# Softmax rows divided after the product with v instead of before it, with the reciprocals spread by way of DRAM

## The chip, the cores and the metric

One NeuronCore of a Trainium2 chip runs the whole program. The metric is device time in microseconds (us) of one execution; a lower time is better. Five engines work side by side, each through its own queue in order: PE (TensorE, matrix products and transposes), DVE (VectorE), ACT (ScalarE), POOL (GpSimd) and SP (SyncE, which here issues every DMA). They wait for each other by semaphores. PE writes to eight PSUM banks; the other engines copy out of them into SBUF, and POOL works on SBUF alone.

## What is computed

Attention with a mask by blocks of 64, a token mixer, a channel mixer and a gated mixer follow each other, on 4 batches of 576 rows and 512 columns (8 heads of 64).

```python
def _attn_ref(q, k, v):
    scores = scale * np.matmul(q, k.transpose(0, 1, 3, 2))
...
    mask = block_i >= block_j
    scores = np.where(mask, scores, -1000000000.0)
    scores = scores - np.max(scores, axis=-1, keepdims=True)
    attn = np.exp(scores)
    attn = attn / (np.sum(attn, axis=-1, keepdims=True) + 1e-09)
    return np.matmul(attn, v).astype(np.float32)

def _moe_ref(x, w_tok1, w_tok2, w_ch1, w_ch2):
    xt = x.transpose(0, 2, 1)
    h = np.maximum(xt @ w_tok1, 0.0) @ w_tok2
    u = x + h.transpose(0, 2, 1)
    h2 = np.maximum(u @ w_ch1, 0.0) @ w_ch2
    return (u + h2).astype(np.float32)

def _moe2_ref(x, mu_k, mu_r, w_k, w_v, w_r):
...
    k = np.maximum(xk @ w_k, 0.0)
    v = k * k @ w_v
    r = 1.0 / (1.0 + np.exp(-(xr @ w_r)))
    return (r * v).astype(np.float32)
```

## The kernel before

**Attention** goes by 16 pairs of heads, p = 0 to 15; four pairs make a batch, and two pairs are one token unit (b, g). For each pair PE computes the scores in three steps (`emit_s`, operands from the tile z, half of the array's rows for each head), and the mask by blocks lets the five row blocks i have 64, 192, 320, 448 and 576 columns (`KE`). For each head h and row block i:

- `m` on DVE (line 389) adds the mask, takes the row maximum and writes the scores to the SBUF tile P;
- `e` on ACT (line 394) takes the exponential in place, and the row sums go to the small tile st;
- `rc` on DVE (lines 398 and 399), four times in a pair, adds 1e-9 to two or three columns of sums and takes the reciprocals;
- `n` on POOL (line 403) multiplies P by the reciprocals, ten times in a pair.

Then PE transposes P in 128x128 pieces, in six groups (`t`, lines 412 and 414; 25 transposes in a pair), ACT or DVE copies each group to a tile pt, and PE multiplies with v in two passes (`pv`, half of the array's columns for each head). Two copies (`q`) bring the result, already with channels on the partitions, into u.

**Token mixer.** For each of the eight units, PE transposes u (`xt`, line 668), ACT and DVE split it into a rounded part and a rest (xnh, xnl), and PE multiplies twice (`k1` by w1, `k2` by w2) with the rectifier between them; `ku` on DVE (line 742) adds the result to u.

**Channel mixer and gated mixer.** Products L and O by w_ch1 and w_ch2 (tiles xhl, hpA, hpB), and then K, R and V (tiles named pair) follow. Their weights are unpacked on ACT, DVE and POOL while the stages before them run; of the pages of w_ch1 and w_ch2 the trace names the raw tiles `raw` and `rawx` and the decoded tiles `td` and `w`.

**What sets the order.** `Plan` takes every step with its engine, a cost, its dependencies and a due time, and records them one by one in the order in which its own reckoning would start them; each engine's queue then holds them in that order. The numbers in the table `TILT` shift the due times by kind of step. Where a step may go to one of two engines (`("ACT", "DVE")`), the plan chooses. Rings limit what is alive at once: `dense` gives three PSUM banks to `pv`, `xt`, `k1` and `k2` together, `pt` two to the transposes of P, `cs` three to the scores.

At the start PE runs twelve products on a zero tile (`warm`), and sixteen more of them (`fill`, tile wz) stand where the plan found PE without other work; all of them are always run.

```python
add(("n", p, h, i), "POOL", 0.31 + 0.00085 * KE[i], [("rc", p, h, g)], ...)
add(("t", p, g), "PE", ..., tprev + [("n", p, h, i) for h, i in need] + ["begin"], ...)
prev = [("q", 4 * b + 2 * g + k, part) for k in range(2) for part in range(2)]   # of xt
```

Of the kernel before, what the change touches and what calls it, by code (L numbers as in the profile page):

```python
# [27 lines left out]
NP = B * H // 2  # L28
# [38 lines left out]
class Plan:  # L67
# [7 lines left out]

    TURNS = {"rc", "d2", "vs", "vs2", "lo", "xm", "xsl", "xT", "Y", "TS", "VL", "KS"}

# [129 lines left out]
def attn_mixer_rwkv_kernel(ctx: ExitStack, tc: tile.TileContext, z, v, vl, wt1, wt2, wc1, wc2, wk, wv, wr, mu, out):  # L207
# [28 lines left out]
    def c_pool2(n):  # L236
        return 0.2 + 0.0023 * n
# [6 lines left out]
    def c_dma(n):  # L244
        return n / 170e3
# [64 lines left out]
    def begin():  # L310
        DVE.memset(f32(wz), 0.0)  # L311
        DVE.memset(eps, 1e-9)
# [17 lines left out]
    plan.ring("z", 2)  # L330
    plan.ring("st", 6)
    plan.ring("cd", 1)
# [12 lines left out]
    def load_v(p):  # L345
        SP.dma_start(out=vs[p % 3], in_=v[p])
        for h in range(2):
            k = slice(64 * h, 64 * h + 64)
            SP.dma_start(out=vd[p % 3][k, :, k], in_=vl[p, k])

# [27 lines left out]
    def p_view(p, h, i):  # L378
        o = (128 * i + 64) * h
        return tl["P", p, i][:, o:o + KE[i]]  # L380

    def emit_max(p, h, i):

        m = mask[:, 0:64] if i == 0 else mask[:, S - KE[i]:S] if h == 0 else mask[:, 512:512 + KE[i]]
        if ("P", p, i) not in tl:
            tl["P", p, i] = pbuf[i][plan.slot[f"P{i}", ("P", p, i)]]
        if ("st", p, h) not in tl:
            tl["st", p, h] = att3.tile([128, 3, 8], F32, tag="st", bufs=6, name="st")
        DVE.tensor_tensor_reduce(p_view(p, h, i), s_view(p, h, i), m, -0.125, 3.0e38, ALU.add, ALU.min,  # L389
                                 tl["st", p, h][:, 0, i:i + 1])  # L390

    def emit_exp(p, h, i):
        st, w = tl["st", p, h], p_view(p, h, i)
        ACT.activation(w, w, ACTF.Exp, bias=st[:, 0, i:i + 1], scale=-1.0, accum_out=st[:, 1, i:i + 1])  # L394
# [26 lines left out]
    def emit_pv(p, chunks):  # L421
        vt, vx = vs[p % 3], vd[p % 3]
        for i in chunks:
            part = int(i == 0)
            if ("pv", p, part) not in tl:
                tl["pv", p, part] = bank(("pv", p, part))
            t, o = tl["pv", p, part], max(0, 128 * i - 128)
            for j in range(i + 1):
                for h in range(2):
                    hs = slice(64 * h, 64 * h + 64)  # L430
                    if j < i:
                        g, c = OFF[h, i, j]
                        mm(t[hs, o:o + 128], vt[:, i - 1 - j if h else j, hs], tl["T", p, g][:, c:c + 128], j == 0, False)
                    else:
                        g, c = DIAG[i]
                        mm(t[hs, o + 64:o + 128] if i else t[hs, 0:64], vx[:, i, hs], tl["T", p, g][:, c:c + 64], j == 0, True)
# [18 lines left out]
    for p in range(NP):  # L455
        w = p - 3
        add(("z", p), "SP", c_dma(128 * 2 * S * 4), ["begin"] if p else [], lambda e, p=p: load_z(p), p - 5, alloc=[("z", ("z", p))], lat=2.0)
# [8 lines left out]
        for h in range(2):  # L466
            for i in range(5):
                step = 2 if i in (1, 2) else (h if i == 4 else 1 - h)
                key = ("c", p, h, {0: 3, 1: 2}.get(i, i))
                f = p - 1.9 + 0.1 * step + 0.03 * {4: 0, 3: 1, 0: 2, 2: 0, 1: 1}[i] + 0.01 * h  # L470
                first = (h, i) in ((0, 4), (1, 3))
                sk, pk = ("st", p, h), ("P", p, i)

                ahead = h == (0 if i in (4, 2, 1) else 1)
                add(("m", p, h, i), "DVE", 0.23 + 0.00104 * KE[i], [("s", p, step)] + ([] if first else [("m", p, h, 4 if h == 0 else 3)]) + ([] if ahead else [("m", p, 1 - h, i)]),
                    lambda e, p=p, h=h, i=i: emit_max(p, h, i), f,
                    alloc=[(f"P{i}", pk)] * ahead + [("st", sk)] * first, uses=[key] + [sk] * (not first) + [pk] * (not ahead))
                add(("e", p, h, i), "ACT", 0.48 + 0.00088 * KE[i], [("m", p, h, i)], lambda e, p=p, h=h, i=i: emit_exp(p, h, i), f, uses=[sk, pk])
                g = 1 if i >= 3 else 0
                add(("n", p, h, i), "POOL", 0.31 + 0.00085 * KE[i], [("rc", p, h, g)], lambda e, p=p, h=h, i=i: emit_norm(p, h, i),  # L480
                    p - 1.4 + 0.1 * (4 - i) + 0.01 * h, uses=[pk, sk])
            for g, (a, b) in enumerate(((0, 3), (3, 5))):
                add(("rc", p, h, g), "DVE", 0.36, [("e", p, h, i) for i in range(a, b)],
                    lambda e, p=p, h=h, a=a, b=b: emit_rec(p, h, a, b), p - 2.5, uses=[("st", p, h)])
# [378 lines left out]

    add("x1", "NONE", 0.0, [("q", NP - 1, 0), ("q", NP - 1, 1)] + [("q", p, k) for p in range(NP) for k in range(2)], change1, -99)
    add("x2s", "NONE", 0.0, ["x1"] + last_tok, change2s, -99)
# [80 lines left out]
    for t in range(NX):  # L946
# [22 lines left out]
        for f in range(12):  # L969
# [11 lines left out]
            def Ll(e, t=t, f=f, w=w):  # L981
# [364 lines left out]
```

## Time and profile before

| what | us |
|---|---|
| median of three executions | 759.02 |
| lowest and highest | 758.59 and 759.62 |
| the profiled execution, its own time | 759.16 |
| its span (first to last instruction) | 757.1 |
| between span and own time | 2.06 |

The profile is of one execution. Busy time is summed by engine; PE's matrix products are pipelined, so that the next starts before the one ahead has ended, and the end that the trace gives is modelled. What a product costs in a row of them is therefore the step from one start to the next, not its own duration. PEld is the load of the operand that stays in the array; it runs beside the products. Idle time of an engine is put down to what ended it (the releaser). A difference of 0.2% of the time, 1.5 us, is about what a measurement of this kernel can tell from none.

### The profile page before, as it was taken

How to read it: one execution, taken by the hardware profiler on the slowest of the kernel's cores; microseconds unless marked ns; L12 is line 12 of the kernel's file. 1: busy time of each engine (PE TensorE's matmuls, PEld its weight loads, DVE VectorE, ACT ScalarE, POOL GpSimd, SP SyncE). 2: the span in 40 equal slices, each digit the busy share in tenths (PEclk: the TensorE clock that was granted, in tenths of full speed). 3: DMA queues.
4: the chain of work that ended last, by engine and by line, in shares of the span. 5: the costliest groups of instructions: out<-in, count | busy, mean ns of one | idle time of the engine just before them, and what ended most of it. 6: DMA issues, size and time to landing. Idle time of an engine off the chain costs nothing.

```text
span 757.1 us, 14545 instructions
## 1 busy us (share of the span) xinstructions
PE 748.8 (99%) x5452; PEld 695.7 (92%) x5452; DVE 532.1 (70%) x1144; ACT 398.9 (53%) x863; POOL 277.7 (37%) x347
## 2 busy tenths in 40 slices
PE   9999999999999999999999999999999999999997
PEld 7888899999999888888888988889999999999997
DVE  5897888878486677557468465112798898897894
ACT  5887775876543461242242422110776775776772
POOL 5776867666475555244144220000120120110210
PEclk9999999999999999999999999999999999999999
DMA  6443544231013542726544550644845955946911
GB/s 197 120 129 115 141 118 153 85 117 58 29 56 134 174 139 83 249 94 221 209 151 169 196 195 29 212 149 156 305 151 189 325 205 186 328 140 186 332 45 48
DMA packets 53237, 119.56 MB, mean 158 GB/s; under 512 B 15408, under 2 KB 19504, under 8 KB 53168
## 3 DMA queue, kind: packets, MB, share of 16 engines
q1 hardware_dynamic: 53168, 118.64, 46.8%
q8 instruction: 43, 0.70, 0.4%
q14 instruction: 26, 0.21, 0.1%
HBM read 94.38 MB, written 24.25 MB: 157 GB/s over the span
## 4 chain that ended last, share of the span: by engine, by line
PE 98%; DVE 1%; POOL 1%; ACT 0%; issue 0%; DVEq 0%; POOLq 0%
PE bank L225 61%; PE pair L225 30%; PE bank L412 5%; PE bank L668 1%; PE bank L414 1%; POOL P L403 1%; ACT pt L215 0%; ACT P L394 0%; DVE u L1266 0%; DVE u L1261 0%; DVE xnl L686 0%; DVE xnh L217 0%; DVE pt L217 0%; DVE wz L311 0%; DVE u L742 0%
## 5 line engine op out<-in xcount | busy, mean ns | idle before, releaser
L225 PE MATMUL pair<-xhl,w 128*128 128x288 f32 x1296 | 176.5, 295 | 0.0
L225 PEld LDWEIGHTS pair<-xhl,w 128*128 128x128 f32 x1296 | 173.7, 188 | 0.6
L225 PE MATMUL bank<-xhl,w 128*128 128x460 f32 (+1 forms) x480 | 104.1, 371 | 0.0
L403 POOL TENSOR_SCALAR P<-P,st 128x448 f32<-128x448 f32 (+4 forms) x160 | 83.8, 546 | 47.5 <-DVE st L399 16.1
L225 PEld LDWEIGHTS bank<-xhl,w 128*128 128x128 f32 x480 | 90.0, 188 | 10.2
L394 ACT ACTIVATE P<-P,st 128x576 f32<-128x576 f32 (+4 forms) x160 | 88.4, 557 | 13.9 <-DVE st L389 13.5
L225 PE MATMUL bank<-hpB,w 128*128 128x460 f32 (+1 forms) x432 | 95.4, 372 | 0.0
L225 PEld LDWEIGHTS bank<-hpB,w 128*128 128x128 f32 x432 | 81.1, 188 | 9.6
L389 DVE CUSTOM_DVE_ANT_0 P<-bank,mask 128x576 f32<-128x576 f32 (+4 forms) x160 | 70.5, 483 | 15.8 <-PE bank L225 13.7
L535 POOL TENSOR_TENSOR td<-td,raw 128x512 int32<-128x512 int32 (+2 forms) x37 | 45.4, 1226 | 68.8 <-DVE td L531 45.9
L979 ACT ACTIVATE hpB<-bank 128x460 fp32r<-128x460 f32 (+1 forms) x36 | 20.0, 556 | 94.0 <-PE bank L225 94.0
L225 PE MATMUL bank<-hpA,w 128*128 128x460 f32 (+1 forms) x288 | 63.9, 371 | 0.0
L225 PEld LDWEIGHTS bank<-hpA,w 128*128 128x128 f32 x288 | 54.0, 188 | 6.2
L982 DVE SCALAR_TENSOR_TENSOR hpB<-bank,hpB 128x460 fp32r<-128x460 f32 (+1 forms) x36 | 22.9, 636 | 49.6 <-ACT hpB L979 49.6
L225 PE MATMUL bank<-z 64*128 64x224 f32 (+4 forms) x448 | 55.3, 376 | 0.0
L982 DVE SCALAR_TENSOR_TENSOR hpA<-bank,hpA 128x460 fp32r<-128x460 f32 (+1 forms) x24 | 15.3, 636 | 55.3 <-ACT hpA L979 55.3
L225 PE MATMUL bank<-xhl,wx 128*128 128x460 f32 (+1 forms) x240 | 53.3, 371 | 0.0
L225 PEld LDWEIGHTS bank<-z 64*128 64x128 f32 x448 | 44.6, 186 | 9.0 <-issue 3.8
L225 PEld LDWEIGHTS bank<-xhl,wx 128*128 128x128 f32 x240 | 45.1, 188 | 5.2
L412 PE MATMUL bank<-ident,P 128*128 128x128 f32 x320 | 49.2, 279 | 0.4 <-DVE pt L217 0.4
L979 ACT ACTIVATE hpA<-bank 128x460 fp32r<-128x460 f32 (+1 forms) x24 | 13.3, 555 | 64.7 <-PE bank L225 64.7
L215 ACT COPY pt<-bank 128x448 f32<-128x448 f32 (+1 forms) x61 | 32.9, 560 | 27.1 <-PE bank L412 12.4
(202 smaller groups left out, 1447.0 us busy)
## 6 DMA issues: line engine op xcount, KB each, us to landing
w<-pages SPq DMA_DIRECT2D x96, 512.0 KB, 4.6
pages<-raw SPq DMA_DIRECT2D x40, 256.0 KB, 2.5
z<-in_z SPq DMA_DIRECT2D x16, 576.0 KB, 3.8
raw<-in_wc SPq DMA_DIRECT2D x18, 512.0 KB, 3.6
pages<-rawx SPq DMA_DIRECT2D x30, 256.0 KB, 2.3
vs<-in_v SPq DMA_DIRECT2D x16, 256.0 KB, 3.8
out<-u SPq DMA_DIRECT2D x14, 288.0 KB, 3.7
rawx<-in_wc SPq DMA_DIRECT2D x6, 512.0 KB, 4.5
```

The source lines that it names most:

```text
L215: ACT.copy(o, i)
L225: PE.matmul(o, lhsT=l, rhs=r, start=start, stop=stop, skip_group_check=more)
L389: DVE.tensor_tensor_reduce(p_view(p, h, i), s_view(p, h, i), m, -0.125, 3.0e38, ALU.add, ALU.min, tl["st", p, h][:, 0, i:i + 1])
L394: ACT.activation(w, w, ACTF.Exp, bias=st[:, 0, i:i + 1], scale=-1.0, accum_out=st[:, 1, i:i + 1])
L403: POOL.tensor_scalar(w, w, tl["st", p, h][:, 2, i:i + 1], 1.0, ALU.mult, ALU.mult)
L412: PE.transpose(t[:, o + 128 * k:o + 128 * k + 128], tl["P", p, i][:, c:c + 128], ident)
L414: PE.transpose(t[:, 64 * k:64 * k + 128], tl["P", p, i][:, 128 * i:128 * i + 128], ident)
L535: POOL.tensor_tensor(td.bitcast(I32), td.bitcast(I32), lw, ALU.add)
L668: PE.transpose(t[0:rows, 256 * k + 128 * p:256 * k + 128 * p + 128], u[b][:, 2 * g + p, c:c + rows], ident)
L979: ACT.activation(tl["h", t, f][0], tl["lb", t, f][:, 0:w], ACTF.Relu)
L982: DVE.scalar_tensor_tensor(tl["h", t, f][1], tl["lb", t, f][:, 0:w], 0.0, f32(tl["h", t, f][0]), ALU.max, ALU.subtract)
```

## The change

P is no longer multiplied by the reciprocals. Transposes of P wait for the exponentials alone. The ten columns of sums of a pair (two heads, five row blocks) lie in one tile st. Once all ten exponentials are done, PE transposes these ten columns (`sx`, one transpose, in a bank of the ring `dense`) into ten rows of 128 numbers; DVE adds 1e-9 and takes the reciprocals (`rc`, lines 405 and 406, 10x128 each); SP writes the ten rows to a DRAM tensor `sums` (`rw`, line 409) and reads them back twice (`rr`, line 415), for each head a row of 576 numbers into 64 partitions of the tile rwide; and u of the pair is multiplied by rwide (`nq`, line 420, 128x576, on POOL or DVE), behind the copies `q`. The token mixer's transposes of u wait for `nq` of both pairs, and so does the start of the channel mixer's buffers (`x1`). To make room, v has two buffers in place of three, and a v load waits for the products of two pairs ahead. Of the numbers in `TILT` nearly all are other ones, so the order changes in all stages; the products L of the first slice keep to four banks from the third on.

```diff
-    eps = att.tile([128, 5], F32, name="eps")
...
-    vs = [att2.tile([128, 4, 128], F32, name=f"vs{s}") for s in range(3)]
-    vd = [att2.tile([128, 5, 128], F32, name=f"vd{s}") for s in range(3)]
+    vs = [att2.tile([128, 4, 128], F32, name=f"vs{s}") for s in range(2)]
+    vd = [att2.tile([128, 5, 128], F32, name=f"vd{s}") for s in range(2)]
+    rrow = [att2.tile([10, 128], F32, name=f"rrow{s}") for s in range(2)]
+    rwide = [att2.tile([128, S], F32, name=f"rwide{s}") for s in range(2)]
...
-    def emit_rec(p, h, a, e):
-        st = tl["st", p, h]
-        DVE.tensor_tensor(st[:, 2, a:e], st[:, 1, a:e], eps[:, a:e], ALU.add)
-        DVE.reciprocal(st[:, 2, a:e], st[:, 2, a:e])
-
-    def emit_norm(p, h, i):
-        w = p_view(p, h, i)
-        POOL.tensor_scalar(w, w, tl["st", p, h][:, 2, i:i + 1], 1.0, ALU.mult, ALU.mult)
+    def emit_row(p):
+        t = tl["sx", p] = bank(("sx", p))
+        PE.transpose(t[0:10, 0:128], tl["st", p][:, 1].rearrange("p h i -> p (h i)"), ident)
+
+    def emit_rec(p):
+        w = tl["rw", p] = rrow[plan.slot["rw", ("rw", p)]]
+        DVE.tensor_scalar(w, tl["sx", p][0:10, 0:128], 1e-9, 1.0, ALU.add, ALU.mult)
+        DVE.reciprocal(w, w)
+
+    def put_rec(p):
+        SP.dma_start(out=sums[p].rearrange("h (i c) -> (h i) c", c=128), in_=tl["rw", p])
+
+    def get_rec(p):
+
+        w = tl["rb", p] = rwide[plan.slot["rb", ("rb", p)]]
+        for h in range(2):
+            SP.dma_start(out=w[64 * h:64 * h + 64], in_=sums[p, h, 64:640].unsqueeze(0).broadcast_to([64, S]))
+
+    def emit_norm(p, e):
+        b, hp = divmod(p, 4)
+        w = u[b][:, hp, 1:1 + S]
+        (POOL if e == "POOL" else DVE).tensor_tensor(w, w, tl["rb", p], ALU.mult)
...
-            add(("t", p, g), "PE", 0.11 * (len(diag) + len(off)), tprev + [("n", p, h, i) for h, i in need] + ["begin"],
+            add(("t", p, g), "PE", 0.11 * (len(diag) + len(off)), tprev + [("e", p, h, i) for h, i in need] + ["begin"],
...
-            prev = [("q", 4 * b + 2 * g + k, part) for k in range(2) for part in range(2)]
+            prev = [("nq", 4 * b + 2 * g + k) for k in range(2)]
...
-                L, p0 + 0.5 * f, alloc=[("dense" if t == 0 else "lo4", key)], uses=[("x", "c", t), ("W", "c1", f)], lat=0.3)
+                L, p0 + 0.5 * f, alloc=[("dense" if t == 0 and f < 2 else "lo4", key)], uses=[("x", "c", t), ("W", "c1", f)], lat=0.3)
```

What the engines' queues hold, at three places. First PE, near the start, in pair 0 (z: scores, ident with P: transposes of P, st: the sums, pt with vs: products with v). Before:

```order
L412 MATMUL bank_128<-ident,P_95 128x128 x4
L412 MATMUL bank_127<-ident,P_95 128x128 x4
L225 MATMUL bank_130<-z 128x288
L225 MATMUL bank_126<-z 128x224
L225 MATMUL bank_130<-z 128x288
L225 MATMUL bank_126<-z 128x224
L225 MATMUL bank_126<-z 128x64
L412 MATMUL bank_124<-ident,P_93 128x128 x3
```

The same queue after, where the sums of pair 0 stand:

```order
L431 MATMUL bank_128<-ident,P_90 128x128
L401 MATMUL bank_129<-ident,st 10x128
L225 MATMUL bank_131<-z 128x288
L225 MATMUL bank_126<-z 128x224
L225 MATMUL bank_131<-z 128x288
L225 MATMUL bank_126<-z 128x224
L225 MATMUL bank_126<-z 128x64
L429 MATMUL bank_125<-ident,P_95 128x128 x4
L225 MATMUL bank_129<-pt_100,vs_108 64x128
```

Before, eight transposes stand together between scores; after, four stand between scores and products with v, and the transpose of the sums ends a visit.

Next DVE, in the pairs 2 to 4 (st: sums, td: unpacking of weights). Before:

```order
L217 COPY pt_98<-bank_125 128x512
L398 TENSOR_TENSOR st<-st,eps 128x3
L399 RECIPROCAL st<-st 128x3
L398 TENSOR_TENSOR st<-st,eps 128x3
L399 RECIPROCAL st<-st 128x3
L389 ISA P_91,st<-bank_126,mask 128x320
```

After, with the multiplication of u of pair 2:

```order
L548 SCALAR_TENSOR_TENSOR td<-raw,td 128x256
L217 COPY u_58<-bank_125 128x512
L217 COPY u_58<-bank_127 128x64
L420 TENSOR_TENSOR u_58<-u_58,rwide_114 128x576
L392 ISA P_90,st<-bank_129,mask 128x320
L392 ISA st 128x1
```

The small steps on the sums are gone from between the maxima, and a multiplication that needs a DMA's result stands ahead of the maxima of pair 4.

Last SP, in the pairs 1 to 3. Before:

```order
L343 DMA z<-in_z 128x1152
L346 DMA vs_110<-in_v 128x512
L349 DMA vd_113<-in_vl 64x5x64 x2
L547 DMA raw<-in_wt 64x256 x2
L346 DMA vs_111<-in_v 128x512
```

After:

```order
L346 DMA z<-in_z 128x1152
L409 DMA sums<-rrow_113 10x128
L415 DMA rwide_115<-sums 64x576 x2
L564 DMA raw<-in_wt 128x256
L349 DMA vs_109<-in_v 128x512
```

A write that waits for DVE, and two reads that wait for this write, now stand ahead of the loads.

## Rows read from the trace of the kernel before

**Rows 1.** The page: span, busy time of each engine, PE's granted clock in 40 slices.
```profile
span 757.1 us, 14545 instructions
...
PE 748.8 (99%) x5452; PEld 695.7 (92%) x5452; DVE 532.1 (70%) x1144; ACT 398.9 (53%) x863; POOL 277.7 (37%) x347
...
PEclk9999999999999999999999999999999999999999
```

**Rows 2.** Busy by stretch: length, then PE, PEld, DVE, ACT, POOL, clock, DMA share, GB/s.
```profile
0.00:216.00 216.00, 212.57 (x2254) 191.87 (x2255) 165.54 (x607) 152.65 (x450) 141.82 (x239) 1.00 0.37 110
```

**Rows 3.** PE in order of time (start, us, what), around its first and last stall.
```profile
18.50 2.10 PE L225 MATMUL bank<-z 64*128 64x320 f32 x18
...
20.53 1.05 PE L412 MATMUL bank<-ident,P 128*128 128x128 f32 x6
21.84 0.55 PE L414 MATMUL bank<-ident,P 128*128 128x128 f32 x3 [0.26 <-POOL P L403]
...
211.97 0.28 PE L225 MATMUL bank<-xnh,w1l 128*128 128x256 f32 x1
212.80 0.39 PE L225 MATMUL bank<-xnh,w1h 128*128 128x256 f32 x1 [0.55 <-DVE u L742]
```

**Rows 4.** PE in order of time from 61.67 to 68.32 us.
```profile
61.67 0.49 PE L412 MATMUL bank<-ident,P 128*128 128x128 f32 x3
61.99 0.27 PE L414 MATMUL bank<-ident,P 128*128 128x128 f32 x1
62.10 0.60 PE L412 MATMUL bank<-ident,P 128*128 128x128 f32 x4
62.46 0.36 PE L225 MATMUL bank<-xnh,w1h 128*128 128x256 f32 x1
62.66 0.28 PE L225 MATMUL bank<-xnl,w1h 128*128 128x256 f32 x1
62.78 0.28 PE L225 MATMUL bank<-xnh,w1l 128*128 128x256 f32 x1
...
65.50 1.23 PE L225 MATMUL bank<-z 64*128 64x288 f32 x10
66.67 0.66 PE L412 MATMUL bank<-ident,P 128*128 128x128 f32 x4
67.26 1.13 PE L225 MATMUL bank<-z 64*128 64x320 f32 x8
68.32 0.88 PE L225 MATMUL bank<-pt,vs 128*64 128x128 f32 x12
```

**Rows 5.** Groups of DVE by shape, and of POOL on the page: busy us, mean ns, idle.
```profile
L398 DVE TENSOR_TENSOR st<-st,eps 128x3 f32<-128x3 f32 x32 | 6.9, 215 | 0.1
L399 DVE RECIPROCAL st<-st 128x3 f32<-128x3 f32 x32 | 5.6, 176 | 1.1
L1046 DVE TENSOR_TENSOR xhl<-raw,xhl 128x576 fp32r<-128x576 f32 x26 | 19.6, 753 | 13.9 <-ACT xhl L215 13.9
...
L403 POOL TENSOR_SCALAR P<-P,st 128x448 f32<-128x448 f32 (+4 forms) x160 | 83.8, 546 | 47.5 <-DVE st L399 16.1
```

**Rows 6.** DMA issues: count, KB each, median us from issue to landing.
```profile
pages<-raw SPq DMA_DIRECT2D x40, 256.0 KB, 2.5
z<-in_z SPq DMA_DIRECT2D x16, 576.0 KB, 3.8
...
out<-u SPq DMA_DIRECT2D x4, 144.0 KB, 1.8
raw<-in_wt SPq DMA_DIRECT2D x2, 128.0 KB, 2.5
mu_sb<-in_mu SPq DMA_DIRECT2D x1, 4.0 KB, 3.5
```

**Rows 7.** The first load of z on PE, in order of time.
```profile
6.75 1.06 PEld L225 LDWEIGHTS bank<-z 64*128 64x128 f32 x10 [0.54 <-issue]
```

More of the change, by code (lines that the diff above doesn't have):

```diff
@@ L311, in begin @@
         DVE.memset(f32(wz), 0.0)
-        DVE.memset(eps, 1e-9)
         DVE.memset(f32(w1l[64:128, 4]), 0.0)
@@ L330, in attn_mixer_rwkv_kernel @@
     plan.ring("z", 2)
-    plan.ring("st", 6)
+    plan.ring("st", 3)
+    plan.ring("rw", 2)
+    plan.ring("rb", 2)
+    sums = nc.dram_tensor("sums", (NP, 2, 640), F32).ap()
     plan.ring("cd", 1)
@@ L345, in load_v @@
     def load_v(p):
-        SP.dma_start(out=vs[p % 3], in_=v[p])
+        SP.dma_start(out=vs[p % 2], in_=v[p])
         for h in range(2):
             k = slice(64 * h, 64 * h + 64)
-            SP.dma_start(out=vd[p % 3][k, :, k], in_=vl[p, k])
+            SP.dma_start(out=vd[p % 2][k, :, k], in_=vl[p, k])
     def s_part(p, h, i, cut):
@@ L386, in emit_max @@
             tl["P", p, i] = pbuf[i][plan.slot[f"P{i}", ("P", p, i)]]
-        if ("st", p, h) not in tl:
-            tl["st", p, h] = att3.tile([128, 3, 8], F32, tag="st", bufs=6, name="st")
+        if ("st", p) not in tl:
+            tl["st", p] = att3.tile([128, 2, 2, 5], F32, tag="st", bufs=3, name="st")
         DVE.tensor_tensor_reduce(p_view(p, h, i), s_view(p, h, i), m, -0.125, 3.0e38, ALU.add, ALU.min,
-                                 tl["st", p, h][:, 0, i:i + 1])
+                                 tl["st", p][:, 0, h, i:i + 1])
     def emit_exp(p, h, i):
-        st, w = tl["st", p, h], p_view(p, h, i)
-        ACT.activation(w, w, ACTF.Exp, bias=st[:, 0, i:i + 1], scale=-1.0, accum_out=st[:, 1, i:i + 1])
-    def emit_rec(p, h, a, e):
-        st = tl["st", p, h]
-        DVE.tensor_tensor(st[:, 2, a:e], st[:, 1, a:e], eps[:, a:e], ALU.add)
-        DVE.reciprocal(st[:, 2, a:e], st[:, 2, a:e])
-    def emit_norm(p, h, i):
-        w = p_view(p, h, i)
-        POOL.tensor_scalar(w, w, tl["st", p, h][:, 2, i:i + 1], 1.0, ALU.mult, ALU.mult)
+        st, w = tl["st", p], p_view(p, h, i)
+        ACT.activation(w, w, ACTF.Exp, bias=st[:, 0, h, i:i + 1], scale=-1.0, accum_out=st[:, 1, h, i:i + 1])
+    def emit_row(p):
[15 more added lines that the diff above has]
+        (POOL if e == "POOL" else DVE).tensor_tensor(w, w, tl["rb", p], ALU.mult)
     def emit_t(p, g):
@@ L421, in emit_pv @@
     def emit_pv(p, chunks):
-        vt, vx = vs[p % 3], vd[p % 3]
+        vt, vx = vs[p % 2], vd[p % 2]
         for i in chunks:
@@ L455, in attn_mixer_rwkv_kernel @@
     for p in range(NP):
-        w = p - 3
+        w = p - 2
         add(("z", p), "SP", c_dma(128 * 2 * S * 4), ["begin"] if p else [], lambda e, p=p: load_z(p), p - 5, alloc=[("z", ("z", p))], lat=2.0)
@@ L470, in attn_mixer_rwkv_kernel @@
                 f = p - 1.9 + 0.1 * step + 0.03 * {4: 0, 3: 1, 0: 2, 2: 0, 1: 1}[i] + 0.01 * h
-                first = (h, i) in ((0, 4), (1, 3))
-                sk, pk = ("st", p, h), ("P", p, i)
+                first = (h, i) == (0, 4)
+                sk, pk = ("st", p), ("P", p, i)
                 ahead = h == (0 if i in (4, 2, 1) else 1)
-                add(("m", p, h, i), "DVE", 0.23 + 0.00104 * KE[i], [("s", p, step)] + ([] if first else [("m", p, h, 4 if h == 0 else 3)]) + ([] if ahead else [("m", p, 1 - h, i)]),
+                add(("m", p, h, i), "DVE", 0.23 + 0.00104 * KE[i], [("s", p, step)] + ([] if first else [("m", p, 0, 4)]) + ([] if ahead else [("m", p, 1 - h, i)]),
                     lambda e, p=p, h=h, i=i: emit_max(p, h, i), f,
@@ L478, in attn_mixer_rwkv_kernel @@
                 add(("e", p, h, i), "ACT", 0.48 + 0.00088 * KE[i], [("m", p, h, i)], lambda e, p=p, h=h, i=i: emit_exp(p, h, i), f, uses=[sk, pk])
[L479 to L484, printed above, removed]
+        sk = ("st", p)
+        add(("sx", p), "PE", 0.11, [("e", p, h, i) for h in range(2) for i in range(5)] + ["begin"], lambda e, p=p: emit_row(p), p - 1.5, alloc=[("dense", ("sx", p))], uses=[sk], lat=0.3)
+        add(("rc", p), "DVE", 0.45, [("sx", p)], lambda e, p=p: emit_rec(p), p - 1.5, alloc=[("rw", ("rw", p))], uses=[("sx", p)])
+        add(("rw", p), "SP", 0.1, [("rc", p)], lambda e, p=p: put_rec(p), p - 1.5, uses=[("rw", p)], lat=2.2)
+        add(("rr", p), "SP", c_dma(128 * S * 4), [("rw", p)], lambda e, p=p: get_rec(p), p - 1.5, alloc=[("rb", ("rb", p))], lat=2.2)
+        add(("nq", p), ("POOL", "DVE"), {"POOL": c_pool2(S), "DVE": 0.75}, [("rr", p), ("q", p, 0), ("q", p, 1)], lambda e, p=p: emit_norm(p, e), p - 0.5, uses=[("rb", p)])
         for g, (diag, off) in enumerate(GROUPS):
@@ L862, in change2s @@
         pools["w2b"] = tc.alloc_tile_pool(name="w2", bufs=1, side="right", reuse_waits="tile")
-    add("x1", "NONE", 0.0, [("q", NP - 1, 0), ("q", NP - 1, 1)] + [("q", p, k) for p in range(NP) for k in range(2)], change1, -99)
+    add("x1", "NONE", 0.0, [("nq", p) for p in range(NP)], change1, -99)
     add("x2s", "NONE", 0.0, ["x1"] + last_tok, change2s, -99)
```

4 lines of the change are left out of this document (2 added, 2 removed).

## The prediction

> **What bounds the kernel now.** I read the page first, then the stretches, then PE in order of time. By the page PE is busy for 748.8 of 757.1 us at the full granted clock in every slice, and no other engine is over 70% [rows 1]. The first 216 us, attention and token mixer, are what the change touches: PE is busy for 212.57 of them, DVE for 165.54, ACT for 152.65, POOL for 141.82 [rows 2]. So the time is PE's work plus the moments in which PE waits, and busy time cannot tell the two apart exactly, because a product's end is modelled. The step from start to start can. Where PE does the same thing twice, the steps repeat to the hundredth, so a longer step is a stall. At 211.97 the step is 0.83 us where its neighbours take 0.12; that is a stall of 0.71, for DVE's update of u, although the row shows only 0.55 as idle. The first one is in the six transposes from 20.53, which wait for POOL's multiplication of P: from 20.53 to 21.84 is 1.31 us, where 0.109 for each makes 0.65 [rows 3]. I found six such stretches between these two (both included) of 0.3 us or more: 0.65 and 0.6 for POOL's multiplication, 1.0 and 0.55 for DVE, 0.3 and 0.8 (with its neighbour steps) at the end of the token mixer. **They sum to 3.9 us**; after 216 us PE runs without one. This is all that a better supply of PE can give back.
>
> **What the change does to PE's own work.** This is where the sum is decided, since PE has nothing spare.
>
> *Prices.* From 61.67 to 62.46 stand eight transposes between token products: 0.79 us, and the product behind them holds the array for 0.20 instead of 0.12, so 0.87, or 0.109 for each, and nothing for the change of kind. From 66.67 to 67.26 stand four between scores: 0.59, where 4 times 0.109 is 0.44. A visit to the transposes from scores (half the rows) or v products (half the columns) thus costs 0.15 more, 0.075 for each edge. Scores in one piece of 18 take 2.03 us (18.50 to 20.53); cut into 10 and 8 they take 1.17 and 1.06, so a cut costs 0.2 [rows 3, 4].
>
> *Counts, from the two orders.* Sixteen transposes of sums are new; their moving operand is ident with 128 columns like that of the others, so 16 x 0.109 = 1.75 us. Edges between transposes and scores or v products go from 31 to 49 on entry and from 34 to 51 on leaving: 35 x 0.075 = 2.6. Pairs whose last two score steps stand together go from nine to five: 4 x 0.2 = 0.8. Against that, pairs whose v product is cut in two go from nine to six, which at the price of a visit gives back 0.45; the filling products stand in five pieces instead of three (+0.15), and the token work in seven pieces fewer (0 to -0.4; I take -0.2). **Together +4.65 us, say 4.7**, on the path, since nothing lies over PE. The sum without the three small terms is 5.15, and with the largest of them 4.45.
>
> **What it takes from the other engines.** POOL's 160 multiplications, 83.8 us, go; DVE's 64 pairs of small steps go, at about 0.2 us a step 23 us in all; in their place come 16 pairs on 10x128 (not shown before; between the 0.17 of a reciprocal on three columns and twice that, so 6 to 11 us) and, by the order, 14 multiplications of u on DVE at 0.753 each, 10.5 us, and two on POOL [rows 5]. All this lies beside PE. What it gives is the two stalls for POOL, 1.25 us; the other four, 2.65, wait for DVE and ACT evictions that stay, and I carry them over. In the sum below all 3.9 are taken off and 2.65 put back.
>
> **The new wait.** The reciprocals now go PE, DVE, DRAM, SBUF, DVE. From the transpose of the sums to landing: about 0.6 for the two small DVE steps and their semaphores; the write; about 0.4 until the second read is issued; the read of 147 KB. The trace has no 5 KB write. The nearest rows are 1.8 (144 KB out, quiet queue), 2.5 (256 KB of pages written to DRAM) and 3.5 (4 KB of mu); for the read 2.5 (128 KB) to 3.8 (576 KB) [rows 6]. That bounds the way to 0.6 + 1.8 + 0.4 + 2.5 = 5.3 and 0.6 + 3.5 + 0.4 + 3.8 = 8.3 us. I take the page write and the 128 KB read, the same direction and size: 0.6 + 2.5 + 0.4 + 2.5 = 6.0. The Trainium skill (DMA: Bandwidth & Descriptors, Anatomy of one DMA) gives about 2.0 us plus bytes over 436 GB/s for one DMA, on the path that GpSimd issues; by that the estimate is 0.6 + 2.0 + 0.4 + 2.3 = 5.3, the lower bound, and the time would be 0.6 us less than below. The 1.8 agrees with it, the 3.5 doesn't.
>
> Who waits: the multiplication stands in DVE's queue, and behind it the maxima of pairs further on, on which the exponentials and the score banks hang. I laid the steps of rows 4 along PE's new order and read when DVE reaches its multiplication: 4.5 us after the sums' transpose for pairs 2 and 15, 5.5 to 6.7 for pairs 0, 1, 6, 8, 10 and 13, and 8 or more for the others. At 6.0 DVE stands for 1.5 us twice and up to 0.5 in two or three more. PE has other pairs' work for about half of that, so it costs 1.0 (0.3 at 5.3 us). The token mixer's transposes come 8.6 us or more behind the sums and are covered below that. SP stands behind the write as well, for some 2.5 us in each pair; behind it are z and v loads, issued about 8 us ahead of use or more, so nothing.
>
> *The start.* PE's first scores wait 0.54 us for z [rows 7], whose load now has the loads of v beside it in place of two weight pages: 0 to -0.5, I take -0.2.
>
> **Sum.** 757.1 + 4.7 - 3.9 + 2.65 + 1.0 - 0.2 = 761.35 us of span. With the 2.06 between span and own time of the profiled execution 763.4; that execution lay 0.14 above the median of the three, so 763.2.
>
> **Rivals.**
>
> *Long way through DRAM.* If write and read come near their upper bounds, 8.3 us, DVE stands 2 to 4 us in eight pairs, 20 us or so in all, and PE passes on a third of it. The 1.0 becomes 6 to 7: 768.5. For it speak vd, z and weights on the same DMA queue, and the 3.5 of the smallest transfer; against it the 1.8. It decides from about 7 us on.
>
> *PE is never late again (not slower).* POOL's ten multiplications stand today between the last exponential and the transposes, so everything behind them is set 2 to 3 us late; with POOL out of the way, evictions may be early too, and only the end of the token mixer (1.1) is left, with 0.5 gained at the start. 757.1 + 4.7 - 3.9 + 1.1 - 0.5 = 758.5 of span, 760.4 by the median: within 0.2%. It decides if the waits sum to less than 1.2 us. Against it: two of the six stalls have DVE as releaser, and DVE and ACT remain at three quarters of the stretch.
>
> *PE is not full.* PEld, the loads of the fixed operand, is busy for only 191.87 of the 216 us [rows 2]. If the 24 us between were hidden waits, the edges would cost nothing and be waits too, and relief on POOL and DVE would shorten them: the 4.7 shrinks to 1.75, the stalls to 1, so 757.1 + 1.75 - 3.9 + 1.0 - 0.2 + 1.9 = 757.7. The Trainium skill (Perfetto Trace Analysis, Identifying the Most-Contended Engine) says that product busy time is no good measure and load busy time is; by that rule PE has this room. The trace speaks against: equal work shows equal steps to the hundredth [rows 4], which waits would not.
>
> That the change doesn't do what it says I leave out: the order shows POOL free of P and the transposes waiting for the exponentials.
>
> **Numbers.** The forecast, 761.5 to 765.5 by its own terms, has 0.60; the long way 0.20; never late 0.14; not full 0.06. About 0.2%, 1.5 us, is what a measurement tells from none, so same is 757.5 to 760.5. Slower: nearly all of the first two and a little of the third, 0.82. Same: 0.13. Faster: 0.05. The range of 8 in 10 reaches into the third and over most of the second: 760.2 to 768.5.
>
> **What would show it.** Right: PE's transposes over scores at 0.59 for four as before; no wait for a reciprocal of P; stalls of PE summing to some 3.5 us, a few of them with DVE's multiplication of u ahead; the sums' way through DRAM near 6 us; 216 us becoming about 220 where the products of the channel mixer begin, and the rest equal. Wrong: a landing beyond 7 us with DVE idle in front of line 420; PE's stalls under 1 us; edges that cost less than 0.075; or a change in length after 220 us, where I see only the same work in a shifted order.

## The result, and the profile after

The changed kernel takes **766.1 us** (median of four) where the kernel before takes 758.8. The medians make 1.0096; the ratio of all executions, 1.0109 (95% interval 1.0071 to 1.0146), is higher because one of the four executions took 770.5 us, at a mean granted clock of 0.995 where the other three, 765.9 to 766.3 us, have 0.998 to 1.000. The forecast was 763.2, slower, with 760.2 to 768.5 as its range. Sign and range hold; 2.9 us of the size are missing.

The page of after, the lines that answer to [rows 1]:

```profile
span 764.1 us, 14377 instructions
...
PE 752.1 (98%) x5468; PEld 695.9 (91%) x5468; DVE 528.2 (69%) x1038; ACT 404.9 (53%) x877; POOL 208.4 (27%) x196
```

The first 216 us of after, to be read beside [rows 2] (length, then PE, PEld, DVE, ACT, POOL busy, clock, DMA share, GB/s):

```profile
0.00:216.00 216.00, 210.26 (x2225) 186.82 (x2226) 162.94 (x501) 156.05 (x460) 58.97 (x78) 1.00 0.44 133
```

POOL is relieved as meant, from 141.8 to 59.0 us. DVE, which lost 64 pairs of small steps, is hardly lighter (165.5 to 162.9). PE, which bounds the kernel, got through 2225 instructions where it did 2254.

To see where the time went, I took PE's steps from start to start together by blocks (a row of products of one kind) and compared each block with what the same block costs where nothing is late; what exceeds that is a stall. The profiled executions then split like this:

| us | before | after | difference | forecast |
|---|---|---|---|---|
| first scores on PE | 6.75 | 6.11 | -0.64 | -0.2 |
| PE's own work to the end of the token mixer | 215.4 | 220.0 | +4.63 | +4.7 |
| stalls of PE in it | 3.87 | 5.15 | +1.28 | -0.25 |
| products of channel and gated mixer | | | +1.44 | 0 |
| from the last product to the end | 4.9 | 5.2 | +0.25 | 0 |
| span | 757.1 | 764.1 | +7.0 | +4.25 |

**PE's work** came as forecast. PE of after in order of time (start, us, what): the four transposes from 21.14 hold the array for 0.58, where the four between scores in [rows 4] hold it for 0.59; the transpose of the sums takes a step of 0.20 ahead of scores.

```profile
19.77 0.27 PE L401 MATMUL bank<-ident,st 128*10 128x128 f32 x1
19.97 1.23 PE L225 MATMUL bank<-z 64*128 64x288 f32 x10
21.14 0.66 PE L429 MATMUL bank<-ident,P 128*128 128x128 f32 x4
21.72 0.88 PE L225 MATMUL bank<-pt,vs 128*64 128x128 f32 x12
```

**The largest stall** is new; by the blocks it is 2.1 us. What PE waited for most in after (total us, times, longest), and PE in order of time around its longest wait:

```profile
PE bank L225 <- DVE st L392: 2.5, 2, 2.0
...
50.98 0.60 PE L429 MATMUL bank<-ident,P 128*128 128x128 f32 x4
53.62 1.24 PE L225 MATMUL bank<-z 64*128 64x288 f32 x10 [2.04 <-DVE st L392]
```

The scores wait for a bank that DVE's maxima (line 392) have not emptied yet. DVE of after in the same microseconds:

```profile
47.37 0.82 DVE L217 COPY u<-bank 128x512 f32<-128x512 f32 x2 [0.22 <-PE bank L225]
50.75 0.76 DVE L420 TENSOR_TENSOR u<-u,rwide 128x576 f32<-128x576 f32 x1 [2.55 <-DMA rwide<-sums]
51.43 0.48 DVE L392 CUSTOM_DVE_ANT_0 P<-bank,mask 128x320 f32<-128x320 f32 x1
```

DVE stood for 2.55 us in front of the multiplication of u of pair 2, and the maxima stood behind it in its queue. In all it stood for 6.9 us there, at the pairs 2, 6, 10 and 15 (total us, times, longest):

```profile
DVE u L420 <- DMA rwide<-sums: 6.9, 4, 2.6
```

**Two stalls of 0.7 us at the end of the token mixer** have another cause. First DVE, then POOL of after, at 208 us:

```profile
208.27 4.42 DVE L420 TENSOR_TENSOR u<-u,rwide 128x576 f32<-128x576 f32 x1 [1.25 <-DMA rwide<-sums]
```

```profile
208.24 3.83 POOL L979 TENSOR_TENSOR xhl<-u,xhl 128x1840 fp32r<-128x1840 f32 x1 [10.93 <-ACT xhl L975]
```

The multiplication that takes 0.76 elsewhere takes 4.42 us. POOL's large subtraction began 0.03 us ahead of it, and DVE ended 0.62 us behind POOL: one after the other, not side by side. DVE's updates of u and the rest h1l, for which PE waits next, came behind it. The Trainium skill (SBUF — State Buffer, SBUF: two separate sides) has the rule: a DVE operation with two SBUF inputs and a GpSimd operation that reads SBUF take a shared pair of ports as an exclusive lock. The trace agrees.

**Behind the token mixer**, PE of after waits once for an update of u, and four times in the gated mixer a product is 0.3 us late; ten products that take 1.89 here take 1.49 where nothing is late:

```profile
246.37 0.79 PE L225 MATMUL bank<-hpA,w 128*128 128x460 f32 x3
247.72 1.53 PE L225 MATMUL bank<-hpA,w 128*128 128x460 f32 x6 [0.56 <-DVE u L759]
...
560.29 1.89 PE L225 MATMUL pair<-hpB,w 128*128 128x288 f32 x10
```

**The way through DRAM.** The small steps on DVE by shape (busy us, mean ns), and the reads (count, KB each, median us from issue to landing), of after:

```profile
L406 DVE RECIPROCAL rrow<-rrow 10x128 f32<-10x128 f32 x16 | 15.1, 941 | 0.6
...
L405 DVE TENSOR_SCALAR rrow<-bank 10x128 f32<-10x128 f32 x16 | 4.4, 276 | 3.3 <-PE bank L401 2.4 <-ACT pt L215 0.8
```

```profile
rwide<-sums SPq DMA_DIRECT2D x32, 144.0 KB, 3.1
```

The trace shows the landing of the second read for seven pairs: 6.5 to 7.9 us behind the start of the sums' transpose in six of them (7.3 at pair 2, 7.9 at pair 10) and 9.4 at pair 5, whose multiplication stands on POOL. The forecast was 6.0, between 5.3 and 8.3. The reciprocal was the term most wrong: 0.94 us where 0.17 to 0.35 was assumed, because [rows 5] show it on three columns and it goes by columns.

The theory after this first look: PE's added work is the largest part (4.6); the rest is DVE standing in front of line 420, its collision with POOL, and the new order of the later stages. Rivals: the way through DRAM is most of it; the order alone is.

### The profile page after: what moved, and what is told of

It reads as the page before. It is cut to its first block, busy times and chain, and to the rows that moved or that the text cites. A ratio compares the mean times of both kernels' runs of the same rounds, so it can differ in the third digit from the quotient of the medians.

```text
span 764.1 us, 14377 instructions
## 1 busy us (share of the span) xinstructions
PE 752.1 (98%) x5468; PEld 695.9 (91%) x5468; DVE 528.2 (69%) x1038; ACT 404.9 (53%) x877; POOL 208.4 (27%) x196
## 4 chain that ended last, share of the span: by engine, by line
PE 86%; DVE 9%; DMA 2%; ACT 1%; issue 1%; SPq 0%; DVEq 0%
PE bank L225 57%; PE pair L225 22%; PE bank L429 5%; DVE rawx L1088 1%; DMA rwide<-sums 1%; PE bank L431 1%; DVE u L420 1%; PE bank L685 1%; DVE wg L1063 1%; DVE P L392 1%; DVE xhl L1063 1%; ACT xhl L215 1%; DVE td L1063 1%; DVE rrow L406 1%; DMA sums<-rrow 0%
## 5 line engine op out<-in xcount | busy, mean ns | idle before, releaser
L225 PE MATMUL bank<-xhl,w 128*128 128x460 f32 (+1 forms) x480 | 106.5, 371 | 0.0
L392 DVE CUSTOM_DVE_ANT_0 P<-bank,mask 128x576 f32<-128x576 f32 (+4 forms) x160 | 69.1, 478 | 12.7 <-PE bank L225 12.5
L215 ACT COPY pt<-bank 128x448 f32<-128x448 f32 (+1 forms) x74 | 40.0, 557 | 34.3 <-PE bank L431 14.8
L429 PE MATMUL bank<-ident,P 128*128 128x128 f32 x320 | 51.1, 280 | 0.5 <-DVE st L392 0.4
L1063 POOL TENSOR_TENSOR xhl<-rawx,xhl 128x576 fp32r<-128x576 f32 x7 | 11.7, 1665 | 129.7 <-DVE raw L1088 88.2
```

The source lines that it names most:

```text
L215: ACT.copy(o, i)
L225: PE.matmul(o, lhsT=l, rhs=r, start=start, stop=stop, skip_group_check=more)
L429: PE.transpose(t[:, o + 128 * k:o + 128 * k + 128], tl["P", p, i][:, c:c + 128], ident)
L1063: (DVE if e == "DVE" else POOL).tensor_tensor(o, a, b, ALU.subtract)
```

## The experiments

Each comparison is with the kernel before, run beside it on the same chip (758.8 to 759.2 us).

**1. Without the way through DRAM** (`e1_no_way`).

```diff
+        for x in rwide:
+            POOL.memset(x, 1.0)
...
-        SP.dma_start(out=sums[p].rearrange("h (i c) -> (h i) c", c=128), in_=tl["rw", p])
+        pass
...
-        for h in range(2):
-            SP.dma_start(out=w[64 * h:64 * h + 64], in_=sums[p, h, 64:640].unsqueeze(0).broadcast_to([64, S]))
```

> The changed kernel without the way through DRAM: the write of the reciprocals and the two reads are not issued, and rwide holds ones from the start, so the rows stay undivided. Every engine keeps its order. Theory (most of the loss is PE's own work in the new order, a part of it DVE standing in front of line 420): the 2.0 us stall of PE at 53.6 and the 0.4 at 156 go, and the last multiplication of u comes clear of POOL's 3.8 us at 208, which gives back the two stalls of 0.7 behind it: 766.1 - 2.5 = 763.6 down to 762.2. Rival 'long way through DRAM' (the way is most of the 7.3): 760 or less. Rival 'only the order counts': 765.5 to 766.5.

Measured: **761.9**, ratio 1.0040 (1.0027 to 1.0052), 4.2 less than the changed kernel and 0.3 under the theory's lower end. The stalls fall from 5.15 to 1.56; the one at 53.6 shrinks from 2.1 to 0.5, those at 156 and at the end of the token mixer are gone. PE's work stays at 220.0. What PE still waited for, in total us, times, longest (the wait for wz is the start):

```profile
PE bank L225 <- DVE wz L312: 1.4, 1, 1.4
PE bank L225 <- DVE st L394: 0.8, 2, 0.4
PE bank L225 <- DVE u L759: 0.6, 1, 0.6
PE bank L225 <- DVE xnl L703: 0.3, 1, 0.3
```

So the way costs 4 of the 7 us, four times the 1.0 that I gave it (the collision at 208 us, 1.4 of stalls, is in it: the last multiplication takes 0.75 here); and without it the kernel is still slower than before.

**2. Also without the transposes of the sums** (`e2_no_sums`).

```diff
-        PE.transpose(t[0:10, 0:128], tl["st", p][:, 1].rearrange("p h i -> p (h i)"), ident)
+        pass
...
-        DVE.tensor_scalar(w, tl["sx", p][0:10, 0:128], 1e-9, 1.0, ALU.add, ALU.mult)
-        DVE.reciprocal(w, w)
+        pass
```

> As the one before, and the sixteen transposes of the sums and DVE's 32 small steps on them are left out too. Theory (PE has nothing spare): 16 x 0.109 = 1.75 us less than without the way, 760.5 to 761.9; what stays over the kernel before, some 2 to 3 us, is the 35 edges and the score cuts. Rival 'PE is not full': within 0.3 us of the kernel without the way.

Measured: **759.9**, 1.0011 (1.0002 to 1.0020), 2.1 less than without the way and 0.6 under the theory's lower end. Where pair 2 had its stall of 2.04, PE now reads:

```profile
50.89 0.60 PE L428 MATMUL bank<-ident,P 128*128 128x128 f32 x4
51.91 1.23 PE L225 MATMUL bank<-z 64*128 64x288 f32 x10 [0.42 <-DVE st L394]
```

PE's work is 217.6 by the blocks, 2.35 less: 16 x 0.109 = 1.75, and most of the rest are visits that a lone transpose of sums had opened (six of the 35 edges, 0.45 by the prediction's price). The stalls are 1.2, far under the 3.87 of before, and still the kernel does not beat it: 2.3 us of edges and cuts and 1.4 in the later stages stand against the 2.7 that the stalls give back. PE's own work is on the path, as the prediction had it.

**3. The way twice as long** (`e3_way_twice`).

```diff
+    sums0 = nc.dram_tensor("sums0", (NP, 2, 640), F32).ap()
...
-        SP.dma_start(out=sums[p].rearrange("h (i c) -> (h i) c", c=128), in_=tl["rw", p])
+        SP.dma_start(out=sums0[p].rearrange("h (i c) -> (h i) c", c=128), in_=tl["rw", p])
+        SP.dma_start(out=sums[p], in_=sums0[p])
```

> The changed kernel with a copy from DRAM to DRAM between write and reads, some 2 to 2.5 us more on the way of each pair. Theory: the multiplications of pairs 0, 1, 2, 6, 8, 10, 13 and 15, which start within 0.8 us of the landing now, come 1.5 to 2.5 us later, 12 to 18 us of DVE standing, of which PE passes on a third: 770 to 773. Rival 'the way is hidden anyway': 766 to 767. Rival 'all of DVE's standing reaches PE': 778 or more.

Measured: **784.3**, 1.0327 (1.0313 to 1.0342): 18 us more than the changed kernel. My "PE passes on a third" fell, and by its time this is the rival's end, at which all of DVE's standing reaches PE. The trace says otherwise. DVE's wait, PE's largest (total us, times, longest) and PE's longest in order of time:

```profile
DVE u L422 <- DMA rwide<-sums: 27.7, 8, 5.1
PE bank L225 <- DVE st L393: 10.1, 7, 4.6
60.52 1.86 PE L225 MATMUL bank<-z 64*128 64x288 f32 x7 [4.60 <-DVE st L393]
```

In the changed kernel DVE's was 6.9 in four times, so it stood for 20.8 us more. PE's waits behind the start grew by 10.5 us, half of that. Most of the rest of the 18 us shows in windows of 2 us (length, PE busy, granted clock, DMA share, GB/s):

```profile
56.00:58.00 2.00, 0.00 (x0) 1.00 0.95 270
58.00:60.00 2.00, 0.00 (x0) 0.53 1.08 289
60.00:62.00 2.00, 1.48 (x7) 0.50 0.35 138
62.00:64.00 2.00, 2.00 (x12) 0.50 0.20 39
64.00:66.00 2.00, 2.00 (x14) 0.77 0.34 121
```

PE stood from 55.9 to 60.5, its longest wait (4.6 us); the granted clock fell from 1.0 to 0.5 (from 2.4 to 1.2 GHz) while PE stood and was back at 65. It is 0.5 at three places (58, 136 and 170 us) for 13.7 us in all, and some 5.5 us of PE's time are lost there (an estimate: half of the stretches in which PE worked). In the profiled execution of the changed kernel the longest wait is 2.0 us, and no stretch of attention or token mixer shows a lower clock.

**4. The last multiplication clear of POOL** (`e4_clear15`).

```diff
             def xl(e, ...):
+                if t == 0 and lo == 0:
+                    POOL.tensor_scalar(one, u[3][:, 3, S:S + 1], 1.0, 1.0, ALU.mult, ALU.mult)
                 POOL.tensor_tensor(l, src, f32(h), ALU.subtract)
```

> The changed kernel with one 128x1 step on POOL ahead of its 128x1840 subtraction (line 979) that reads the divided u of pair 15, so that this subtraction starts behind the last multiplication of u instead of beside it. Theory (the two engines hold each other up): the multiplication takes 0.76 instead of 4.42 us, the two stalls of 0.7 us at the end of the token mixer go: 764.4 to 765.2. Rival 'the 4.42 us are late data or a record's error': unchanged, 766 to 766.5. Rival 'the subtraction is awaited': slower by up to 0.8 us.

The collision is settled by the trace, the time is not. DVE, then POOL:

```profile
209.88 0.76 DVE L421 TENSOR_TENSOR u<-u,rwide 128x576 f32<-128x576 f32 x1 [2.15 <-DMA rwide<-sums]
```

```profile
211.06 3.86 POOL L982 TENSOR_TENSOR xhl<-u,xhl 128x1840 fp32r<-128x1840 f32 x1
```

The multiplication takes 0.76 again, and the two stalls of 0.7 are gone. But the median is **766.0**, 1.0086 (1.0072 to 1.0099), unchanged: in the profiled execution (765.0) the reads of pairs 2 and 15 landed 0.4 and 0.9 us later behind their sums' transposes, DVE stood for 11.6 us in front of its multiplications instead of 6.9, and the stall at 53.6 was 2.5 instead of 2.1. The other three executions, 765.9 to 766.3, have a mean granted clock of 0.996 where the profiled one has 0.998; they were not profiled, so what they lost to the clock isn't shown. By the time the rival "unchanged" can't be told from the theory.

**5. The kernel before without its division** (`e5_before_no_norm`).

```diff
-        POOL.tensor_scalar(w, w, tl["st", p, h][:, 2, i:i + 1], 1.0, ALU.mult, ALU.mult)
+        pass
...
-        DVE.tensor_tensor(st[:, 2, a:e], st[:, 1, a:e], eps[:, a:e], ALU.add)
-        DVE.reciprocal(st[:, 2, a:e], st[:, 2, a:e])
+        pass
```

> The kernel before without its division: POOL's 160 multiplications and DVE's 64 small steps on the sums are left out, the order stays. This is the most that moving the division away from P can give. Theory: the two stalls behind POOL (0.65 and 0.62) go, and of the two behind DVE (1.0 and 0.56) some part, since DVE has 12.5 us less to do: 759.2 - 1.3 = 757.9, down to 756.6. Rival 'PE is never late again': 756.5 or less. Rival 'POOL is off the path': 759 to 759.5.

Measured: **758.0**, 0.9986 (0.9977 to 0.9995). A division that costs nothing at all is worth 1.3 us as long as the order of before is kept; a change that adds 4.6 us to PE could not have won by that. It is no bound for a new order: run 10 gains more. DVE became 19.7 us lighter (532.1 to 512.4), not the 12.5 that I expected, which counts the steps on three columns alone.

**6. The later stages in their old order** (`e6_later_order`): in `TILT` the numbers of the kernel before for all kinds of the channel and gated mixers.

> The changed kernel with the numbers of the kernel before in TILT for all kinds of the channel mixer and the gated mixer; attention and token mixer keep theirs, and PE's order is the same up to the last product of the token mixer but six. Theory (the 1.4 us that came in behind the token mixer are the later stages' new order): 766.1 - 1.4 = 764.7, between 764.2 and 765.2. Rival 'they follow from the division': 766 to 766.5.

Measured: median **766.0**, 1.0103 (1.0085 to 1.0121), the five between 765.0 and 769.1; the median doesn't show the gain. The blocks do: the products of the two mixers take what they take in the kernel before, to 0.1 us, and the ten products of 560 us read

```profile
560.70 1.49 PE L225 MATMUL pair<-hpB,w 128*128 128x288 f32 x10
```

In exchange the stalls ahead of them were 0.7 us longer in this execution (2.5 instead of 2.1 at pair 2, and 0.6 new at 230). The five differ in clock too: the two at a mean granted clock of 1.000 took 765.0 and 765.4 us, the two longest (769.1 and 767.7) have 0.994 and 0.997. That the later order makes the 1.44 is shown in the trace; the median lies where the rival wanted it, and the time alone would not have decided.

**7. No transpose of the sums on PE** (`e7_no_transpose`): DVE takes the reciprocals on 128x10, the write to DRAM turns them.

```diff
-        SP.dma_start(out=sums[p].rearrange("h (i c) -> (h i) c", c=128), in_=tl["rw", p])
+        SP.dma_start(out=sums[p].rearrange("h (i c) -> c h i", c=128), in_=tl["st", p][:, 0])
```

> The changed kernel without the transpose of the sums: DVE takes the reciprocals in the tile st (128x10), and the write to DRAM turns them, element by element, 1280 of 4 bytes in each pair. Order as it was. PE loses 16 transposes; without the way that was worth 2.1 us. DVE's two steps should take about 0.4 instead of 1.2 us, so the way is 1 us shorter if the write takes as long as the old one: 762 to 763.5. If the write by elements takes 2 us longer, the way is 1 us longer than now, and by the run with the doubled way the time goes up by some 8 us: 770 to 774. Both ends are open; the trace tells which by the time between the write's issue and the reads'.

Measured: **869.1**, 1.1459 (1.1444 to 1.1475), far beyond both ends. The write:

```profile
sums<-st SPq DMA_DIRECT2D x16, 5.0 KB, 9.3
```

1280 elements of 4 bytes take 9.3 us to land; DVE stands for 92.7 us in front of line 420, and PE's mean granted clock is 0.942. The Trainium skill (DMA: Bandwidth & Descriptors, Anatomy of one DMA) would give 2.0 us for 5 KB, on the path that GpSimd issues. The measurement decides. It is not the bytes: in run 3 the copy of 5 KB from DRAM to DRAM landed in 1.9 us. That the number of pieces makes the difference is what remains, but no run varied it.

**8. All multiplications of u on POOL** (`e8_on_pool`), same order.

```diff
-        (POOL if e == "POOL" else DVE).tensor_tensor(w, w, tl["rb", p], ALU.mult)
+        POOL.tensor_tensor(w, w, tl["rb", p], ALU.mult)
```

> The changed kernel with all sixteen multiplications of u on POOL, at the same places of the order; nothing else moves. The wait for the reads then stands in POOL's queue and no longer ahead of DVE's maxima. Theory (PE is late because DVE stands in front of line 420, not because the result comes late): the stalls of PE fall to what they are without the way, 5.15 to about 1.6 us: 766.1 - 3.6 = 762.5, between 761.9 and 763.3. Rival 'the way itself is late for the token mixer': no less than 765. Rival 'POOL's unpacking of weights is held up instead': 766 or more.

Measured: **761.9**, 1.0043 (1.0030 to 1.0056), the same as with no way at all. POOL waits instead:

```profile
POOL u L420 <- DMA rwide<-sums: 48.9, 9, 14.2
```

Stalls of PE: 1.43 instead of 5.15. This settles it: the way through DRAM is not too long; it was waited for in the wrong queue. The collision goes with it, since both of its operations now follow each other on POOL.

**9. Planned anew** (`e9_pair_order`); besides `TILT` and the durations below, the plan's price for a change of kind (`SWITCH`) is 0.089 in place of 0.09 and its bonus for staying with one kind of product 0.107 in place of 0.25.

```diff
-        add(("rc", p), "DVE", 0.45, ...
+        add(("rc", p), "DVE", 1.2, ...
-        add(("rw", p), ..., lat=2.2)
+        add(("rw", p), ..., lat=2.4)
-        add(("rr", p), ..., lat=2.2)
+        add(("rr", p), ..., lat=2.6)
```

> The changed kernel planned anew: the plan is told what the trace shows (1.2 us for the reciprocals in place of 0.45, a longer way through DRAM), the numbers in TILT are other ones, those of the later stages are the kernel before's. Nine of sixteen multiplications of u stand on POOL, the others late on DVE. By the prices of steps PE's work is 219.6 us (220.0 in the changed kernel, 215.4 before), the later order gives back 1.4, and the stalls fall to about 2: 766.1 - 0.4 - 1.4 - 3.2 = 761.1, between 759.5 and 762. Theory: still slower than the kernel before, since the edges and the transposes of sums remain. Rival 'only the order was bad': 759 or less.

Measured: **760.5**, 1.0022 (1.0013 to 1.0030). Work 219.4, stalls 1.2. As a change by pairs it remains 1.6 us behind the kernel before.

**10. Two pairs together** (`e10_two_pairs`), planned anew: the sums wait for the exponentials of both pairs, the plan's bonus for staying with one kind of product is 0 in place of 0.25, and its price for a change of kind 0.054 in place of 0.09.

```diff
-            tl["st", p] = att3.tile([128, 2, 2, 5], F32, tag="st", bufs=3, name="st")
+            tl["st", p // 2] = att3.tile([128, 2, 2, 2, 5], F32, tag="st", bufs=2, name="st")
...
-        DVE.tensor_scalar(w, tl["sx", p][0:10, 0:128], 1e-9, 1.0, ALU.add, ALU.mult)
+        w = tl["st", p][:, 1]
+        DVE.tensor_scalar(w, w, 1e-9, 1.0, ALU.add, ALU.mult)
         DVE.reciprocal(w, w)
+    def emit_rows(p, e):
+        w = tl["rw", p] = rrow[plan.slot["rw", ("rw", p)]]
+        copy(e, w, tl["sx", p][0:20, 0:128])
...
-        PE.transpose(t[0:10, 0:128], tl["st", p][:, 1].rearrange("p h i -> p (h i)"), ident)
+        PE.transpose(t[0:20, 0:128], tl["st", p][:, 1].rearrange("p r h i -> p (r h i)"), ident)
```

> A new version: the sums of the two pairs of a token unit go together, in eight transposes of twenty columns instead of sixteen of ten; the reciprocals are taken ahead of the transpose, on 128x20, and the transposed rows are only copied (ACT or DVE); fourteen of the sixteen multiplications of u stand on POOL; the order is planned anew for few edges, with the kernel before's numbers for the later stages. By the prices of steps PE's work is 216.7 us (220.0 in the changed kernel, 215.4 before), the stalls should be about 1.1 and the later order gives back 1.4: 766.1 - 3.3 - 4.0 - 1.4 = 757.4, between 756.3 and 758.6, faster than both kernels. Rival 'every version with the division behind the product pays on PE': 759.2 or more.

Measured: **754.9**, 0.9948 (0.9934 to 0.9961), 4 us faster than the kernel before and 11 than the changed one. The only wait of PE that its trace names is the start's, and the reciprocals have become small (DVE by shape):

```profile
PE bank L226 <- DVE wz L313: 1.4, 1, 1.4
```

```profile
L407 DVE RECIPROCAL st<-st 128x20 f32<-128x20 f32 x8 | 2.2, 278 | 0.3
```

It came out 2.5 us better than expected, 1.4 below the range. From start to start PE spends 216.4 us on attention and token mixer, 1.0 more than the work of the kernel before; no stall is named behind the start, where I expected 1.1. The sums in pairs, the reciprocals ahead of the transpose, the multiplications on POOL and the new order came together here, and no run parts them.

**11. A control** (`e11_before_order`): the kernel before with numbers in `TILT` from the same search.

> A control: the kernel before, planned anew by the same search over the numbers in TILT as the new version with two pairs (the same count of trials, the same measure). By the prices of steps PE's work stays at 215.4 us, and the stalls may fall by up to 0.7. Theory (the new version's gain comes from its smaller work on PE and the free way, not from the search alone): 758.0 to 759.2. Rival 'any newly planned order gains as much': 756 or less.

Measured: **758.5**, 0.9998 (0.9989 to 1.0007). The search over `TILT` alone gives nothing here. The control kept the plan's bonus and price for a change of kind, which run 10 changed; whether the kernel before, or the one of run 5, would gain by these is not tested.

| | first scores | PE's work | stalls | time |
|---|---|---|---|---|
| before | 6.75 | 215.4 | 3.9 | 759 |
| after | 6.11 | 220.0 | 5.2 | 766.1 |
| 1 no way | 6.87 | 220.0 | 1.6 | 761.9 |
| 8 on POOL | 6.86 | 220.0 | 1.4 | 761.9 |
| 2 no way, no sums | 6.22 | 217.6 | 1.2 | 759.9 |
| 9 pairs, new order | 6.32 | 219.4 | 1.2 | 760.5 |
| 10 two pairs | 6.82 | 216.4 | none named | 754.9 |
| 5 before, no division | 6.86 | 215.4 | 2.9 | 758.0 |

## Why the prediction was right, and where not

*Sign and main term: right.* The 4.7 us of PE's own work came as 4.63, from prices in [rows 4] and counts of the two orders. Its two parts hold as well: with six edges the transposes of the sums were priced at 2.2 and measure 2.35 (run 2), the other edges and the cuts at 2.5 and measure 2.3. Run 2 shows the work on the path: stalls of 1.2 and still no gain. The rival "PE is not full" fell with run 10, where PE waits for nothing behind the start and PEld still reads

```profile
0.00:216.00 216.00, 214.56 (x2250) 192.78 (x2251) 159.24 (x515) 147.48 (x438) 77.36 (x93) 1.00 0.48 137
```

192.8 of 216, 0.9 more than in [rows 2]. The time in which no weights are loaded was no room to wait less. The rule of the Trainium skill that I set against the trace (Perfetto Trace Analysis, Identifying the Most-Contended Engine), to judge TensorE's headroom by load busy time, would have found 23 us here.

*Stalls: two errors that partly cancelled.* I carried 2.65 us of old stalls over; without the way 1.56 are left (run 1), so the relief was larger than I took. And the term for DVE's waiting was 1.0, where runs 1 and 8 show 3.6 of stalls. Four steps in it failed. The reciprocals were sized from three columns, 0.6 us too short. DVE stood for 6.9 us (pairs 2, 6, 10 and 15), where the working had 1.5 twice and up to 0.5 in two or three more, 3 to 4.5 in all. The 1.0 was not even half of that: "other pairs' work for about half" makes 1.5 to 2.2 of it. The half itself, a guess without a row, held in run 3, where 10.5 of 20.8 us of standing became waits of PE, but less well at pair 2, where a wait of 2.55 made 1.6 of the stall of 2.1 (0.5 is there without the way too, run 1). And the meeting of the last multiplication with POOL's subtraction I did not look for: 1.4 us. That the stalls missed the forecast by no more than 1.5 us is luck.

*The start*: 0.64 instead of 0.2, but the runs scatter from 5.9 to 6.9 with the same order ahead of it, so this is no effect of the change that these runs could show.

*Behind 220 us*: I said that there was "only the same work in a shifted order", and named a change in length as what would make me wrong. It came, 1.44 us; run 6 traces it to the new numbers for the later stages, without which the division does as well.

*Sum*: 1.53 too little for stalls, 1.44 for the later stages, 0.25 for the tail, less 0.45 for the start, make the 2.75 by which the span was missed.

*Rivals.* "Long way through DRAM" was to decide from 7 us on; the way was 6.5 to 7.9 where DVE waited for it, and half of its price was paid. The sign of being wrong that I had named, a landing beyond 7 us with DVE idle in front of line 420, came at the pairs 2 and 10; the lower bound of 5.3 was never reached. The rival's price went by a third of DVE's standing where the forecast went by a half. "PE is never late again" was right on the size (about 1.2 to 1.6 of stalls) once the wait left DVE, in runs 1, 2, 8 and 9, but not for the change as made.

What stays open: how much of the 1.4 of the collision the time would show by itself (run 4), how the 2.3 us of edges and cuts in run 2 divide, since no run changed them alone, and which of the four changes of run 10 its gain comes from.

## What to carry to other kernels

A wait for a slow way costs what stands behind it in the same queue: put the waiting instruction on an engine whose queue has time (here POOL: 4.2 us for one word, the end of the collision included). Where one engine is full, count its own instructions and changes of kind before its stalls: in a given order, a relief elsewhere is worth no more than the stalls that it ends, and leaving the relieved work out altogether (run 5) tells that bound in one run. A new order can pass it: run 10 gained 4 us where run 5 had shown 1.3. Give a planner measured durations: the changed kernel's reckons with 0.45 us for reciprocals that take 1.2.

## What the runs showed of the hardware

A reciprocal on DVE goes by columns and is dear: 10x128 takes 941 ns, 128x20 278, 128x10 216 (run 7), 128x3 176. From 10 to 20 columns each further one takes 6.2 ns, from 20 to 128 6.1. The same 1280 sums cost less than a quarter if they are taken before the transpose (128x10 against 10x128).

A DVE operation with two SBUF inputs beside a large POOL operation took 4.42 us instead of 0.76. A write of 5 KB in 1280 pieces took 9.3 us to land. And a wait of PE of 4.6 us cost more than itself: the granted clock was 0.5 when PE went on and stayed there for some 4.4 us more.
